# An attention and two-MLP kernel on one core: four query halves with whole float32 weights, a hand-set start, and a new order

## The chip, the cores and the metric

The kernel runs on one core of one Trainium2 chip. The metric is the device time of one execution in microseconds (us). Engines are named as in the profile: PE is TensorE (PEld its weight loads), DVE VectorE, ACT ScalarE, POOL GpSimd, SP SyncE, which here only issues DMAs. Each engine works through its own instructions strictly in the order in which they stand; semaphores hold an instruction until what it reads is there.

## The reference

Sixteen attention problems (2 batches of 8 heads, 768 positions, 64 channels), with a mask made by clustering, then two MLPs over the 1536 tokens:

```
q_assign = argmax(normalised q . normalised centroids)     # 16 clusters a head; the same for k
scores   = where(q_assign == k_assign, q . k / 8, -1e9)
attn     = exp(scores - rowmax) / (rowsum + 1e-9)
x        = attn . v                       # 1536 tokens x 512
x        = elu(x . w_in) . w_out          # 512 -> 2048 -> 512
out      = ((x . w_a) * (x . w_b)) . w_out2     # 512 -> 1536 -> 512
```

Inputs and output are float32. The kernel keeps near-float32 precision by splitting operands into a high and a low part and multiplying the parts. The MLP weights arrive as float64 bits and are made into two float32r parts by steps `wa`, `w0` to `w4`, `wh`, `ws`, `wq`.

## The kernel before

The program is one long table, `ORDER`: each word is a step with its arguments, and the steps are issued in the order of the words. A word such as `tr:0.1.0/tt=1` also names the buffer it takes. So the order of the words is, engine by engine, the order of the instructions; nothing is scheduled at run time.

Heads go in pairs `j` (heads 2j and 2j+1). Queries of a head lie in six tiles `t` of 128; tiles 0 to 2 are half `f`=0, tiles 3 to 5 half 1. For each pair and tile:

- `lk`, `lp`, `lq` load keys, paired queries and single queries; `ka1`, `ka2`, `kb`, `qa`, `qb` make the float32r operands of the scores.
- `sm` multiplies queries and keys with the centroids in plain float32 (12 small products a pair); `m1` to `m5` turn the result into one-hot rows on DVE; `ot`/`oe` (pair 0) or `oh`, `ohs`, `ohd` (the others) put them into rows 64 to 80 of `kb` and `qb`, so that the mask comes out of the score product itself. Ahead of the first `sm` the centroids are loaded (`cn`), normalised (`c0`, `c1`, `c2`), transposed (`c3`) and laid out in blocks (`c4`).
- `sc` makes the scores of one tile (four matmuls of 384 columns), `rm` their row maximum on DVE, `ex` the exponentials on ACT, with row sums. The result `pf` is float32.
- The weights must then be transposed. On one of two paths: `tr` (three PE transposes) with `th`, which copies the transposed tile out of PSUM as a float16 high part, and `tl`, which subtracts for the low part; or `hi` and `lo`, which split `pf` ahead, and `td`, one DMA transpose of both parts. Split tiles go through a ring of four `phl` buffers.
- `av` multiplies with the values in three parts of 12 matmuls: high by high, low value by high, high value by low, 36 matmuls of 384 columns a half, the two heads in the two halves of the array's columns. `v1` and `v2` are the float16 parts of the values. `ra`, `rc`, `rx`, `rb`, `re` bring 1/sum into place and `ev` scales.

`vl` and `vr` load the values and scan them for their largest magnitude. `wm` issues eight warming products of 128 columns that nothing reads. The MLP steps (`h`, `x2`, `ab`, `o` on PE) follow the last attention pair; the first of them, `h:0.0.0`, stands in the table while the last pair is finished.

`av` of half `f` is held by every transposed tile of both heads of that half; `sc` by a free score buffer (two of them), so by `ex` two tiles ago.

Of the kernel before, what the change touches and what calls it, by code (L numbers as in the profile page):

```python
# [76 lines left out]
hi:0.2.1/phl=0 vs:3 w0:1 qb:3.0 sc:1.1/sc=1 wm:54 sc:1.0/sc=0 th:0.0.1.1/pt=0 wm:50 w1:1 kbd:2
lq:6.0/rawq=0 th:0.1.0.1 w2:1 rm:1.1/nm=3 wh:1 lo:0.2.2 rm:1.0/nm=0 ex:1.1/pf=0 ex:1.0/pf=2 wm:59
wm:44 wm:12 tl:0.1.0 vs:1 sc:1.2/sc=1 tr:0.1.1/tt=1 v1:2.1/v1=0 w3:1 lp:2.0/rawp=0 hi:1.1.2/phl=1
lo:1.1.2 sc:0.3/sc=0 v1:1.1/v1=1 wm:9 ws:1 tl:0.0.1 rm:1.2/nm=1 lq:4.0/rawq=1 vs:0 th:0.1.1.0 td:0.2  # L80
ex:1.2/pf=1 rm:0.3/nm=2 tl:0.1.1 tr:1.0.0/tt=0 wm:36 sc:0.5/sc=1 th:0.0.0.1 ex:0.3/pf=0/sum=1 wm:34
tr:1.0.1/tt=1 hi:1.2.1/phl=2 sc:0.4/sc=0 tl:0.0.0 rm:0.5/nm=3 th:1.0.0.1/pt=1 w4:1 tl:1.0.0
# [1076 lines left out]
```

## Time and profile before

| | us |
|---|---|
| median of 3 timed runs | 803.97 (801.41 to 805.08) |
| the profiled execution's own time | 803.56 |
| its span, first to last instruction | 801.8 |
| busy in the span: PE / DVE / ACT / POOL | 786.2 / 580.0 / 414.1 / 355.5 |

The span falls into three stages. Up to the first score matmul operands are loaded and made. Then all four compute engines work on the attention. From the first MLP product on, PE has matmuls back to back. A busy PE is not a PE at its peak, since each matmul's record holds its latency too; what PE has to spare is read from how closely its records follow each other.

### The profile page before, as it was taken

To read this page: it belongs to the slowest core of one execution; us is meant where nothing else is said; L and a number is where in the kernel's file an instruction comes from. 1 tells how busy PE (TensorE), PEld (TensorE's weight loads), DVE (VectorE), ACT (ScalarE), POOL (GpSimd) and SP (SyncE) were. 2 spreads that over 40 slices of the span, in tenths; PEclk is the share of its full clock that TensorE was granted. 3 is DMA by queue.
4 is the path that set the end of the run, shared out by engine and by line. 5 is a ranking of instruction groups with operands and counts; after the bars stand their busy time and mean duration, and the time that the engine had idled before them with its cause. 6 is when DMAs were issued, how large, how long until landed. Compare 5 with 4: busy or idle time off the path is not lost.

```text
span 801.8 us, 11888 instructions
## 1 busy us (share of the span) xinstructions
PE 786.2 (98%) x4474; PEld 645.2 (80%) x4474; DVE 580.0 (72%) x838; ACT 414.1 (52%) x717; POOL 355.5 (44%) x290
## 2 busy tenths in 40 slices
PE   9999999999999999999999999999999999999998
PEld 9877777777778878888888888888888888888886
DVE  4899998899998676987887788874258873565222
ACT  7889998899986443652742654331223323132110
POOL 0688877979853234445444422540133522332000
PEclk9999999999999999999999999999999999999999
DMA  9577999989941113223213220221012211110102
GB/s 311 156 170 165 204 153 202 217 187 159 158 120 46 60 53 105 75 84 104 78 56 105 80 78 27 81 77 54 1 53 76 79 57 52 53 54 0 53 1 105
DMA packets 98009, 79.12 MB, mean 99 GB/s; under 512 B 81248, under 2 KB 81248, under 8 KB 97952
## 3 DMA queue, kind: packets, MB, share of 16 engines
q1 hardware_dynamic: 97648, 77.58, 38.5%
q10 hardware_dynamic: 304, 0.79, 0.3%
q8 instruction: 35, 0.57, 0.3%
q14 instruction: 22, 0.18, 0.1%
HBM read 51.41 MB, written 3.15 MB: 68 GB/s over the span
## 4 chain that ended last, share of the span: by engine, by line
PE 82%; issue 5%; DVE 4%; ACT 3%; DMA 3%; POOL 2%; SPq 1%; POOLq 0%; ACTq 0%; DVEq 0%
PE ab L942 8%; PE ab L943 8%; PE ab L941 8%; PE sc L689 6%; PE x L941 5%; PE h L941 5%; PE h L943 5%; PE x L943 5%; PE h L942 5%; PE x L942 5%; PE o L942 4%; PE o L943 4%; PE o L941 4%; PE av L802 4%; PE tt L743 2%
## 5 line engine op out<-in xcount | busy, mean ns | idle before, releaser
L697 DVE TENSOR_REDUCE nm<-sc 128x1 f32<-128x768 f32 x96 | 90.6, 949 | 6.8 <-PE sc L689 6.3
L725 POOL TENSOR_TENSOR phl<-pf,phl 128x768 f16<-128x768 f32 x49 | 84.2, 1723 | 22.1 <-ACT phl L718 12.7
L710 ACT ACTIVATE pf<-sc,nm 128x768 f32<-128x768 f32 x96 | 86.9, 905 | 10.1 <-DVE nm L697 7.2
L1043 ACT COPY t0ab<-ab 128x512 f32<-128x512 f32 x36 | 21.1, 587 | 109.2 <-PE ab L943 109.2
L1048 DVE TENSOR_TENSOR t1ab<-ab,t0ab 128x512 f32<-128x512 f32 x36 | 24.8, 689 | 63.2 <-ACT t0ab L1043 63.2
L689 PE MATMUL sc<-ka,qa 128*128 128x384 f32 x192 | 59.3, 391 | 4.3 <-ACT pf L710 3.8
L872 ACT ACTIVATE wg<-wraw 128x512 f32<-128x512 f32 x68 | 45.0, 667 | 26.8 <-DMA wraw<-in_w_out_dram 14.4
L802 PE MATMUL av<-pt,v 128*64 128x384 f16 x576 | 54.9, 334 | 0.6 <-DMA qb<-ohs 0.6
L889 DVE SCALAR_TENSOR_TENSOR wf<-wraw,wg 128x512 int32<-128x512 int32 x68 | 51.5, 760 | 1.8
L689 PE MATMUL sc<-kb,qb 80*128 80x384 f32 x192 | 51.0, 347 | 0.4 <-DMA kb<-ka 0.4
L752 DVE TENSOR_TENSOR pt<-tt,pt 128x384 f16<-128x384 f32 x92 | 48.6, 544 | 2.5 <-ACT pt L747 2.3
L902 DVE SCALAR_TENSOR_TENSOR wg<-wraw,wg 128x512 f32<-128x512 uint32 x68 | 49.2, 724 | 1.5
L1059 DVE TENSOR_TENSOR gl<-t1ab,gh 128x512 fp32r<-128x512 f32 x36 | 33.9, 941 | 18.7 <-ACT gh L1054 18.5
L743 PE MATMUL tt<-identf,pf 128*128 128x128 f32 x276 | 44.2, 281 | 2.9 <-DVE pt L752 2.6
L802 PEld LDWEIGHTS <-v 128*64 128x64 f16 x576 | 31.2, 111 | 19.0 <-issue 8.0
L877 DVE TENSOR_SCALAR wg<-wg 128x512 f32<-128x512 f32 x68 | 39.3, 578 | 8.1 <-ACT wg L872 8.0
L689 PEld LDWEIGHTS sc<-ka,qa 128*128 128x128 f32 x192 | 30.1, 195 | 14.5 <-ACT pf L710 11.8
L743 PEld LDWEIGHTS tt<-identf,pf 128*128 128x128 f32 x276 | 32.3, 143 | 11.6 <-DVE pt L752 2.0
L882 DVE TENSOR_SCALAR wg<-wg 128x512 int32<-128x512 int32 x68 | 38.4, 566 | 1.8
L1005 ACT CAST gh<-t1h 128x1024 fp32r<-128x1024 f32 x24 | 25.2, 1052 | 27.6 <-DVE t1h L997 27.6
L997 DVE SCALAR_TENSOR_TENSOR t1h<-t0h,h 128x1024 f32<-128x1024 f32 x24 | 29.2, 1216 | 13.1 <-ACT t0h L992 13.1
L1099 DVE TENSOR_TENSOR acc<-o,acc 128x1024 f32<-128x1024 f32 (+1 forms) x12 | 14.2, 1180 | 32.3 <-PE o L943 32.3
(375 smaller groups left out, 2347.2 us busy)
## 6 DMA issues: line engine op xcount, KB each, us to landing
wraw<-in_w_out_dram SPq DMA_DIRECT2D x28, 512.0 KB, 3.3
wraw<-in_w_in_dram SPq DMA_DIRECT2D x16, 512.0 KB, 3.6
wraw<-in_w_a_dram SPq DMA_DIRECT2D x12, 512.0 KB, 3.5
wraw<-in_w_b_dram SPq DMA_DIRECT2D x12, 512.0 KB, 3.5
rawq<-in_qt_dram SPq DMA_DIRECT2D x30, 192.0 KB, 3.8
rawp<-in_qt_dram SPq DMA_DIRECT2D x8, 384.0 KB, 4.4
acc<-in_v_dram SPq DMA_DIRECT2D x4, 768.0 KB, 11.0
rawk<-in_kt_dram SPq DMA_DIRECT2D x7, 384.0 KB, 5.1
```

What stands on the lines that cost most here:

```text
L689: nc.tensor.matmul(s[:, j, :HALF], a[:, qs], b[:, j * HALF : (j + 1) * HALF], start=i == 0, stop=i == 1,)
L697: nc.vector.reduce_max(out=nm, in_=st[g][f"sc{t}"][:, :, :HALF], axis=AX.XY, negate=True)
L710: nc.scalar.activation(pf.rearrange("p (a b) -> p a b", a=2), st[g].pop(f"sc{t}")[:, :, :HALF], AF.Exp, bias=st[g].pop(f"nm{t}"), accum_ou ...
L725: (nc.vector, None, nc.gpsimd)[e].tensor_sub(phl[:, S:], st[g].pop(f"pf{t}"), phl[:, :S])
L743: nc.tensor.transpose(tt[:, k * P : (k + 1) * P], pf[:, o : o + P], identf)
L752: nc.vector.tensor_sub(lo, st[g].pop(f"tt{t}{u}"), hi)
L802: nc.tensor.matmul(pairs[j]["av"][x * 64 : (x + 1) * 64].rearrange("p (a q) -> p a q", a=3), st[2 * j + x][("v1", "v2")[vi]][:, kt_, :], s ...
L889: nc.vector.scalar_tensor_tensor(out=f, in0=raws[n][:, :, 1], scalar=-0x40000000, in1=g, op0=ALU.bitwise_and, op1=ALU.bitwise_or,)
L902: nc.vector.scalar_tensor_tensor(out=g, in0=raws.pop(n)[:, :, 0].bitcast(U32), scalar=2.0 ** -52, in1=g, op0=ALU.mult, op1=ALU.mult,)
L941: nc.tensor.matmul(ps, lhi, rhi, start=first, stop=False)
L942: nc.tensor.matmul(ps, lhi, rlo, start=False, stop=False)
L943: nc.tensor.matmul(ps, llo, rhi, start=False, stop=last)
```

## The change

- The start of the table is set by hand: the centroid chain comes first, and 12 of the 60 warming steps are left (5 ahead of the first score step where there were 44, 7 behind it where there were 16). Of the 16 value scans, which all stood ahead of the first score step, 13 now stand behind it.
- For the halves in `WHOLE`, that is half 0 of pairs 1, 3, 4 and 6, the transposed weights are kept as one float32 tile. There `th` copies float32, `tl` falls away, all tiles go through PE, and a new step `aw` multiplies them in plain float32 with the float32 values in `acc`: 12 matmuls a half in place of 36. Half 1 of the same pairs sends all six tiles through the DMA transposes.
- `ra` has a second form, on DVE. Casts and other splits move between ACT, DVE and POOL.
- All steps up to the first MLP block stand in a new order.

Counts over the whole table, before and after: `tl` 92 and 52, `tr` and `th` 92 and 100, `hi`, `lo` and `td` 50 and 46, `av` 48 and 36, `aw` 0 and 12, `wm` 60 and 12. By engine: `lo` on POOL 49 and 38, on DVE 1 and 8; `hi` on ACT 38 and 30, on DVE 0 and 5; `qa` on ACT 16 and 9, on POOL 0 and 6; `ra` on ACT 16 and 6, on DVE 0 and 10. From `h:0.0.0` on the products are the same.

```diff
+WHOLE = {(1, 0), (3, 0), (4, 0), (6, 0)}
 ORDER = """
-lk:0.1/rawk=0 wm:0 wm:2 lp:0.0/rawp=0 lq:1.1/rawq=0 cz:0 lq:0.0/rawq=1 ib:0 wm:4 wm:6 cs:0 wm:7
...
+lk:0.1/rawk=0 lp:0.0/rawp=0 wm:0 cs:0 c0:0 md:0 lq:0.1/rawq=0 wm:2 wm:4 c1:0 wl:0 ce:0 ka1:1.1 wa:0
...
     def pt_of(g, f):
         if f"pt{f}" not in st[g]:
-            st[g][f"pt{f}"] = take(ap, "pt", [P, 3, 2 * NT, P], F16, f"pt{f}_{g}", 4)
+            shape, dt = ([P, 3, NT, P], F32) if (g // 2, f) in WHOLE else ([P, 3, 2 * NT, P], F16)
+            st[g][f"pt{f}"] = take(ap, "pt", shape, dt, f"pt{f}_{g}", 4)
         return st[g][f"pt{f}"]
...
     @op
-    def ra(j, f):
+    def ra(j, f, e):
         s = pairs[j]["rs", f] = take(ap, "rs", [P, 16], F32, f"rs_{j}_{f}", 2)[:, :6]
-        nc.scalar.activation(s, flat(pairs[j]["sum", f]), AF.Identity, bias=eps)
+        if e:
+            nc.scalar.activation(s, flat(pairs[j]["sum", f]), AF.Identity, bias=eps)
+        else:
+            nc.vector.tensor_scalar_add(s, flat(pairs[j]["sum", f]), 1e-9)
...
+    @op
+    def aw(j, f, n):
+        if n == 0:
+            pairs[j]["av"] = take(psumA, "av", [P, HALF], F32, f"av_{j}_{f}")
+        for kt_ in (2 * n, 2 * n + 1):
+            for x in range(2):
+                g = 2 * j + x
+                nc.tensor.matmul(
+                    pairs[j]["av"][x * 64 : (x + 1) * 64].rearrange("p (a q) -> p a q", a=3),
+                    staged(g)[:, kt_ * D : (kt_ + 1) * D], st[g][f"pt{f}"][:, :, kt_, :],
+                    start=kt_ == 0, stop=kt_ == NT - 1,
+                )
```

On DVE the centroid chain (`csq`, `cnorm`, `cn`, then `cblk`) stood behind the cast of the identity and a split of keys that waits for ACT. Before:

```order
L408 CAST identb<-identf 128x128
L565 TENSOR_TENSOR ka_243<-rawk_111,ka_243 64x768
L371 TENSOR_TENSOR csq<-cn 128x64
L372 TENSOR_REDUCE cnorm<-csq 128x1
L384 TENSOR_SCALAR cnorm<-cnorm 128x1
L385 RECIPROCAL cnorm<-cnorm 128x1
L386 TENSOR_SCALAR cn_104<-cn,cnorm 128x128
L508 SCALAR_TENSOR_TENSOR qb_304<-rawq_131,qa_291 64x768
L565 TENSOR_TENSOR ka_227<-rawk_111,ka_227 64x768
L508 SCALAR_TENSOR_TENSOR qb_341<-rawq_135,qa_314 64x768
L401 COPY cblk<-cps 64x4x16 x2
```

The same place of DVE after:

```order
L368 TENSOR_TENSOR csq<-cn 128x64
L369 TENSOR_REDUCE cnorm<-csq 128x1
L381 TENSOR_SCALAR cnorm<-cnorm 128x1
L382 RECIPROCAL cnorm<-cnorm 128x1
L383 TENSOR_SCALAR cn_104<-cn,cnorm 128x128
L405 CAST identb<-identf 128x128
L398 COPY cblk<-cps 64x4x16 x2
L562 TENSOR_TENSOR ka_165<-rawk_111,ka_165 64x768
```

The chain is now first, and one cast stands between its scaling and its blocks.

On ACT, at the first exponentials (`pf<-sc`), the value scans (`junk,vmax<-acc`) all stood ahead. Before:

```order
L455 ACTIVATE junk,vmax<-acc 128x384 x6
L558 CAST ka_544<-rawk_455 64x768
L455 ACTIVATE junk,vmax<-acc 128x384 x4
L671 CAST kb_245<-ot_570 16x768
L583 ACTIVATE qa_604<-rawq_513 128x768
L872 ACTIVATE wg_669<-wraw_534 128x512
L583 ACTIVATE qa_674<-rawq_343 128x768
L710 ACT_TABLE_LOAD
L710 ACTIVATE pf_0_677,sum_0_676<-sc_0_622,nm_0_672 128x768
```

ACT at its first exponentials after:

```order
L668 CAST kb_178<-ot_261 16x768
L452 ACTIVATE junk,vmax<-acc 128x384 x3
L707 ACTIVATE pf_0_310,sum_0_309<-sc_0_272,nm_0_298 128x768
L452 ACTIVATE junk,vmax<-acc 128x384
L707 ACTIVATE pf_0_341,sum_0_309<-sc_0_286,nm_0_330 128x768
L452 ACTIVATE junk,vmax<-acc 128x384 x8
L707 ACTIVATE pf_0_409,sum_0_309<-sc_0_375,nm_0_406 128x768
```

Three, one and eight scans now stand around the first three exponentials; the table load has gone further ahead.

On PE, at the products of weights and values of pair 1 half 0 (heads 2 and 3, `pt_2`, `pt_3`), a part was 12 loads and matmuls of float16. Before:

```order
L783 MATMUL rbp_0_1423<-identf,rx_0_1417 128x128 x3
L802 LDWEIGHTS v_2_826
L802 MATMUL av_0_1436<-pt_2_1178,v_2_826 64x384
L802 LDWEIGHTS v_3_1043
L802 MATMUL av_0_1436<-pt_3_1252,v_3_1043 64x384
L802 LDWEIGHTS v_2_1208
```

The same place of PE after, the end of one part and the start of the next:

```order
L818 MATMUL av_0_1051<-pt_3_892,acc 64x384
L785 MATMUL rbp_0_1060<-identf,rx_0_1056 128x128 x3
L686 MATMUL sc_4_1067<-ka_575,qa_632 128x384 x2
L686 MATMUL sc_4_1067<-kb_785,qb_673 128x384 x2
L686 MATMUL sc_4_1084<-ka_575,qa_632 128x384 x2
L686 MATMUL sc_4_1084<-kb_785,qb_673 128x384 x2
L818 MATMUL av_0_1051<-pt_2_776,acc 64x384
```

A part is now four plain float32 matmuls, and scores of pair 2 stand between the parts.

## Rows read from the trace of the kernel before

**Rows 1.** Windows: the stages; busy us (records) by engine, clock, DMA share, GB/s

```profile
0.00:27.20 27.20, 25.75 (x395) 24.91 (x396) 14.06 (x29) 19.06 (x46) 5.70 (x32) 1.00 0.89 293
27.20:236.40 209.20, 199.71 (x1580) 157.10 (x1578) 195.86 (x314) 192.13 (x384) 166.88 (x133) 0.98 0.86 170
300.00:400.00 100.00, 100.00 (x443) 82.81 (x442) 79.13 (x104) 48.15 (x61) 47.52 (x33) 1.00 0.27 86
```

**Rows 2.** Timeline, the first MLP product: start us, duration us, instruction

```profile
236.45 0.48 PE L941 MATMUL h<-x0h,w0h 128*128 128x512 f32 x1
```

**Rows 3.** Timeline, the start: PE, DVE and SP up to the first scores

```profile
0.75 0.40 SPq L354 DMA_DIRECT2D cn<-in_cent_dram  x1
...
1.20 11.09 PE L433 MATMUL warm_ps<-warm 128*128 128x128 bf16 x168 [1.20 <-DVE eps L348]
...
1.35 0.77 DVE L408 CAST identb<-identf 128x128 bf16<-128x128 f32 x1 [0.20 <-POOL identf masks.py:199]
...
7.57 0.23 DVE L371 TENSOR_TENSOR csq<-cn 128x64 f32<-128x64 f32 x1
...
8.70 0.29 DVE L386 TENSOR_SCALAR cn<-cn,cnorm 128x128 f32<-128x128 f32 x1
...
12.12 0.28 PE L395 MATMUL cps<-identf,cn 128*128 128x128 f32 x1
...
12.23 3.74 PE L433 MATMUL warm_ps<-warm 128*128 128x128 bf16 x64
12.51 0.46 DVE L401 COPY cblk<-cps 64x64 f32<-64x64 f32 x2 [0.54 <-PE cps L395]
...
15.81 0.36 PE L602 MATMUL tp<-cblk,rawp 128*128 128x32 f32 x2
...
20.18 0.69 DVE L902 SCALAR_TENSOR_TENSOR wg<-wraw,wg 128x512 f32<-128x512 uint32 x1
...
23.56 0.95 DVE L667 TENSOR_SCALAR qb<-ot 16x768 fp32r<-16x768 bf16 x1 [1.03 <-PE ot L659]
...
27.28 0.59 PE L689 MATMUL sc<-ka,qa 128*128 128x384 f32 x2
```

**Rows 4.** DMA issues of the start: KB each, us from issue to landing

```profile
cn<-in_cent_dram SPq DMA_DIRECT2D x1, 32.0 KB, 3.4
```

**Rows 5.** Groups by line, DVE, 0 to 236.4 us: busy us, mean ns | idle before

```profile
L752 DVE TENSOR_TENSOR pt<-tt,pt 128x384 f16<-128x384 f32 x84 | 44.5, 544 | 0.5 <-ACT pt L747 0.3
...
L767 DVE RECIPROCAL rs<-rs 128x6 f32<-128x6 f32 x15 | 2.7, 181 | 0.0
...
L877 DVE TENSOR_SCALAR wg<-wg 128x512 f32<-128x512 f32 x6 | 2.6, 440 | 0.7 <-ACT wg L872 0.7
...
L725 DVE TENSOR_TENSOR phl<-pf,phl 128x768 f16<-128x768 f32 x1 | 0.9, 939 | 0.0
```

**Rows 6.** Groups by line, ACT, 0 to 236.4 us

```profile
L718 ACT CAST phl<-pf 128x768 f16<-128x768 f32 x38 | 31.6, 832 | 0.3
L583 ACT ACTIVATE qa<-rawq 128x768 fp32r<-128x768 f32 x16 | 13.4, 843 | 0.0
```

**Rows 7.** Groups by line, POOL, 0 to 236.4 us

```profile
L725 POOL TENSOR_TENSOR phl<-pf,phl 128x768 f16<-128x768 f32 x49 | 84.2, 1723 | 22.1 <-ACT phl L718 12.7 <-issue 8.3
...
L718 POOL CAST phl<-pf 128x768 f16<-128x768 f32 x12 | 11.9, 992 | 6.1 <-issue 2.9 <-ACT pf L710 2.8 <-POOL phl L725 0.4
```

**Rows 8.** Chain that ended last, pieces of PE: start us, us

```profile
39.54 0.33 PE tt L743 x3
...
68.17 2.60 PE tp L602 x24
...
124.87 1.10 PE av L802 x12
```

**Rows 9.** Windows, two microseconds behind a `tp` run, columns as in Rows 1

```profile
98.00:100.00 2.00, 2.00 (x13) 0.99 (x13) 1.59 (x3) 1.47 (x4) 1.70 (x2) 0.50 1.07 249
```

**Rows 10.** DMA issues, the transposes: count, us from issue to landing

```profile
pt<-phl SPq DMA_TRANSPOSE x50, 4.2
```

More of the change, by code (lines that the diff above doesn't have):

```diff
@@ L77 @@
[L77 to L82, printed above, removed]
@@ new lines @@
+hi:0.2.1/phl=0 wm:25 vtd:0 ex:1.0/pf=1 kbd:2 ka1:3.2 sc:1.1/sc=1 wa:1 rm:1.1/nm=0 lo:0.2.2
+vbp:0/tt=2 ex:1.1/pf=0 sc:1.2/sc=0 tr:1.0.1/tt=1 vbd:0 sm:1/tt=2 qa:2.1 td:0.2 th:1.0.1.1/pt=1
+th:0.0.1.1 w0:1 rm:1.2/nm=1 vs:0 w1:1 lk:2.0/rawk=0 sc:0.3/sc=1 hi:1.1.1/phl=1 ex:1.2/pf=2 qb:2.0
+sc:0.5/sc=0 w2:1 tl:0.0.1 m1:1/mx=1 rm:0.3/nm=2 lo:1.1.2 vs:1 rm:0.5/nm=3 m2:1 v1:0.1/v1=0
+hi:1.2.1/phl=2 ex:0.3/pf=0/sum=1 m3:1 tr:1.0.0/tt=0 m4:1 v1:1.1/v1=1 ex:0.5/pf=1 lo:1.2.2
+sc:0.4/sc=1 th:1.0.0.1 sc:1.3/sc=0 hi:0.5.1/phl=3 vs:3 rm:0.4/nm=0 lp:2.0/rawp=0 tl:1.0.1
@@ new lines @@
+tl:1.3.1 tr:1.3.0/tt=2 th:0.4.1.1 lq:5.0/rawq=1 tl:0.4.0 hi:1.5.1/phl=2 w4:1 ex:2.0/pf=0/sum=0
+ra:0.1.0/rs=1 v1:2.1/v1=2 ex:2.1/pf=1 lo:1.5.2 sc:2.2/sc=1 tl:0.4.1 rm:2.2/nm=2 wl:2 th:1.3.0.0
+tr:2.0.0/tt=0 tr:2.1.1/tt=1 sc:3.0/sc=0 rx:0.0/rx=0 ka1:5.1 th:2.0.0.1/pt=0 lk:4.0/rawk=1 wq:1
+rb:0.0/tt=0 kbd:4 th:2.1.1.1 ex:2.2/pf=2 tr:2.0.1/tt=1 sc:3.1/sc=1 ka2:5.2 re:0.0.1/rb=0
+tr:2.1.0/tt=0 rm:3.0/nm=3 tl:1.3.0 rc:0.1 ev:0.0 ex:3.0/pf=0 wa:2 rm:3.1/nm=0 th:2.0.1.1 td:1.5 w0:2
+rx:0.1/rx=1 tr:2.2.1/tt=2 th:2.1.0.0 ex:3.1/pf=1 sc:3.2/sc=0 tr:2.2.0/tt=1 th:2.2.0.1 w1:2 kbd:5
@@ new lines @@
+ohd:4 th:7.2.1.1 hi:6.4.2/phl=3 td:6.3/pt=2 ev:2.1 th:7.0.0.0 kbd:10 hi:6.5.1/phl=1 rm:7.3/nm=0
+aw:3.0.0 lo:6.4.2 rm:7.5/nm=3 ex:7.3/pf=1 td:6.4 sc:7.4/sc=1 ex:7.5/pf=0 v2:7.2/v2=3 lp:6.0/rawp=1
+sc:8.0/sc=0 th:7.0.1.1 qa:10.2 lo:6.5.2 hi:7.3.1/phl=0 rx:3.0/rx=0 rm:7.4/nm=2 rm:8.0/nm=1
+ex:7.4/pf=2 vs:11 aw:3.0.1 lo:7.3.0 sc:8.1/sc=1 w4:3 hi:7.4.1/phl=2 ex:8.0/pf=1/sum=0 aw:3.0.2
+ra:3.1.0/rs=1 lo:7.4.2 hi:7.5.1/phl=3 sc:8.2/sc=0 tr:8.0.1/tt=1 v1:8.1/v1=1 rc:3.1 tr:8.0.0/tt=2
+td:6.5 rm:8.1/nm=0 qa:11.0 vs:10 ex:8.1/pf=2 th:8.0.1.1/pt=3 rb:3.0/tt=0 lo:7.5.2 rm:8.2/nm=3
@@ new lines @@
+sc:10.0/sc=0 v2:10.2/v2=1 rm:10.0/nm=1 ex:9.4/pf=2 ka1:12.1 td:8.4 sc:10.1/sc=1 ra:4.1.0/rs=1
+aw:4.0.2 ex:10.0/pf=0/sum=0 lo:9.3.2 re:4.0.1/rb=0 rc:4.1 rm:10.1/nm=0 lq:13.0/rawq=0 sc:10.2/sc=0
+tr:10.0.0/tt=1 ex:10.1/pf=1 w1:4 tr:10.0.1/tt=2 hi:9.4.0/phl=0 rm:10.2/nm=3 th:10.0.0.1/pt=2
+lo:9.4.2 rx:4.1/rx=1 sc:11.0/sc=1 td:8.5 tl:10.0.0 td:9.5/pt=1 tr:10.1.1/tt=0 th:10.0.1.1 td:9.3
+ex:10.2/pf=0 th:10.1.1.1 rm:11.0/nm=2 v2:9.2/v2=2 hi:10.2.2/phl=2 tr:10.1.0/tt=1 sc:11.1/sc=0
+tl:10.0.1 ex:11.0/pf=2 rm:11.1/nm=1 rb:4.1/tt=2 re:4.1.1/rb=1 sc:11.2/sc=1 rm:11.2/nm=0 sm:6/tt=2
@@ new lines @@
+th:10.1.0.1 lo:10.2.2 ev:4.0 v2:11.2/v2=3 ex:11.1/pf=1 hi:11.1.1/phl=3 lo:11.1.2 tl:10.1.0 tl:10.1.1
+ex:11.2/pf=0 hi:11.2.1/phl=1 sc:10.3/sc=0 m1:6/mx=0 td:9.4 ra:5.0.0/rs=0 qa:13.1 m2:6 tr:11.0.0/tt=1
+lk:7.0/rawk=0 sc:10.4/sc=1 tr:11.0.1/tt=0 lo:11.2.2 ka1:13.1 rm:10.3/nm=3 rm:10.4/nm=2 ka2:13.2
+ex:10.3/pf=1/sum=1 m3:6 m4:6 m5:6/oht=0 av:4.1.0 sc:10.5/sc=0 ex:10.4/pf=2 th:11.0.0.1/pt=3 qb:13.0
+sc:11.3/sc=1 rm:11.3/nm=1 hi:10.4.1/phl=0 th:11.0.1.1 oh:6/tt=2 td:10.2 rm:10.5/nm=0 ohs:6/ohs=1
@@ new lines @@
+kbd:12 ex:11.3/pf=0 lo:10.4.2 av:4.1.1 av:4.1.2 td:11.1 ka1:14.2 tr:10.3.0/tt=2 ka2:12.2
+ex:10.5/pf=2 tl:11.0.1 rc:5.0 th:10.3.0.1/pt=0 td:11.2 ohd:6 ev:4.1 sc:11.4/sc=1 tl:11.0.0
+tr:10.3.1/tt=0 sc:11.5/sc=0 rm:11.4/nm=3 av:5.0.0 rm:11.5/nm=2 td:10.4 hi:10.5.1/phl=2
+tr:11.3.1/tt=1 lo:10.5.2 tl:10.3.0 ex:11.4/pf=1 sc:12.0/sc=1 tr:11.3.0/tt=2 th:10.3.1.1 w2:4
+rm:12.0/nm=1 hi:11.4.1/phl=3 lo:11.4.2 tl:10.3.1 av:5.0.1 ex:11.5/pf=2 w3:4 ka2:14.2
+ex:12.0/pf=0/sum=0 th:11.3.1.0/pt=1 lp:7.0/rawp=0 sc:12.1/sc=0 ra:5.1.1/rs=1 rm:12.1/nm=0
@@ new lines @@
+tl:14.0.0 rm:15.0/nm=1 hi:14.2.2/phl=3 th:14.0.1.1 re:6.0.1/rb=0 tr:14.1.0/tt=0 ex:15.1/pf=2
+tr:14.1.1/tt=2 v2:15.2/v2=1 lo:14.2.2 td:13.4 td:13.5 th:14.1.0.1 v2:14.2/v2=3 tl:14.0.1 tl:14.1.0
+sc:15.2/sc=0 ev:6.0 rx:6.1/rx=1 tr:15.1.1/tt=1 rm:15.2/nm=0 ex:15.0/pf=1 th:14.1.1.1 tr:15.1.0/tt=0
+wl:5 sc:14.3/sc=1 th:15.1.1.1/pt=3 av:6.1.0 ex:15.2/pf=0 av:6.1.1 tl:15.1.1 tr:15.0.1/tt=1
+rm:14.3/nm=3 hi:15.2.0/phl=1 sc:14.4/sc=0 th:15.1.0.1 tl:15.1.0 ra:7.0.1/rs=0 tl:14.1.1 th:15.0.1.0
+rc:7.0 lo:15.2.2 ex:14.3/pf=2/sum=1 tr:15.0.0/tt=0 sc:15.3/sc=1 rb:6.1/tt=2 wh:4 tl:15.0.1
@@ L733, in parts_of @@
         f, a = divmod(t, 3)
+        parts = 1 if (g // 2, f) in WHOLE else 2
         return [pt_of(g, f)[:, a, i * NT + 3 * u : i * NT + 3 * (u + 1)].rearrange("p m q -> p (m q)")
-                for i in range(2)]
+                for i in range(parts)]
     @op
```

374 lines of the change are left out of this document (167 added, 207 removed).

## Prediction

> **What bounds the kernel now.** I read the windows by stage first, then the timeline of the start, then the groups by line of each engine, and last the chain of waits for PE's pace. The reader is to see three stages. From the first MLP product at 236.45 us [rows 2] PE has 443 matmuls in every 100 us [rows 1], 0.226 us each, with no gap; these products stay as they are, so what the change gains or loses is how much earlier or later that product starts. From 27.2 to 236.4 us DVE is busy 195.9 of 209.2 us, 93.6%, ACT 91.8%, POOL 79.8% [rows 1]. DVE is the bound there, with ACT close behind. In the first 27.2 us DVE is busy only 14.06 us and ACT 19.06 [rows 1]: that stage is a chain of waits, and 13.1 us of DVE's time are lost in it.
>
> PE shows 199.7 of 209.2 us busy in the attention, but that counts latency. By pace: a score matmul of 384 columns is 0.226 x 384/512 = 0.169 us, a step of three transposes 0.33, an `av` part 1.10, an `sm` 2.60 [rows 8], eight warming products 3.74/8 = 0.47 [rows 3]. From the first score to the first MLP product the table holds 384 score matmuls (65 us), 87 transpose steps (29), 45 `av` parts (49.5), 7 `sm` (18), 15 `rb` at the price of a transpose step (5) and 16 warming steps (7.5): 174 of 209 us, 83%. PE has slack.
>
> **The start.** Today the centroid chain begins at 7.57 us although its data land at 0.75 + 3.4 = 4.15 us [rows 3, 4], because DVE first waits with a split of keys. It then stands before PE, which works off 168 warming products until 12.1 us; the transposed centroids come at 12.12, the blocks are done at 12.97, and `sm` starts only at 15.81, behind 64 more warming products [rows 3]. From there to the first score are 27.28 - 15.81 = 11.47 us.
>
> After: the chain from its load takes 8.70 + 0.29 - 7.57 = 1.42 us to the scaled centroids, 0.28 for the transpose, 0.77 for the cast of the identity that still stands in the way on DVE, 0.46 for the blocks: 4.15 + 2.93 = 7.1 us for `sm`. The 40 warming products left ahead of it end earlier. From `sm` to the first score I take today's 11.47 less two pieces of DVE that now stand behind it, one mask row of `qb` (0.95) and one weight step (0.69) [rows 3]: 9.8 us. First score at 16.9, say 17, where it was 27.3. But work is moved too: DVE's 14.06 us ahead of the score fall to about 10.1 (a split and an operand at 0.95 each, the two pieces above, and 0.4 of the small steps on the value scale). So DVE's idle time at the start falls from 13.1 to 17 - 10.1 = 6.9 us: the start is worth 6.2 us, not 10.
>
> **Work taken off the attention, counted in the table up to `h:0.0.0`.**
> - DVE: 38 `tl` fewer at 0.544 = -20.7; 7 `lo` more at 0.939 = +6.6; 6 `th` more at `tl`'s price (same tile, same PSUM read) = +3.3; 9 `ra` at `rc`'s 0.18 (same six columns) = +1.6; 5 `hi` = +3.3, for which there is no row on DVE: 440 ns for 512 columns gives 0.66 for 768, the split's 0.939 is the upper end, and I take the first as the nearer kind [rows 5]. Six single steps that come or go make about -0.5. Sum -6.4 us.
> - ACT: 8 `hi` at 0.832 and 7 `qa` at 0.843 are 12.6 us less [rows 6]; the moved sums and casts take off some 3 more.
> - POOL: 11 `lo` fewer at 1.723 = -19.0; 6 `qa` more, unseen on POOL, between the cast's 0.99 and the split's 1.72, at 0.99 since it too reads one operand: +6; other moves +1.7. Sum -11 [rows 7].
> - PE: 9 transpose steps more (+3.0), 12 `av` parts less (-13.2), 9 warming steps less behind the first score (-4.2), and `aw`.
>
> `aw` has no row. Twelve plain float32 matmuls of 384 columns a half; the only plain float32 product in the trace, `sm`, shows its 12 as 24 records [rows 8], so 24 records a half. Lower end: a record as cheap as one of `av`, 1.10/12 = 0.092, so 2.2 us a half, 1.1 less than the 3.3 of three `av` parts. Upper end: four column times a record and the two heads one after the other, 24 x 4 x 0.169 = 16.2 us. I take two column times, between one and four, and the heads side by side, as `av`'s row shows it (0.092 against 0.169): 24 x 2 x 0.169/2 = 4.1 us, 0.8 more than today, +3 us in all. PE's sum is then 65 + 31.7 + 36.3 + 18 + 5 + 3.3 + 16.2 = 175 us. Nothing bounds there.
>
> The Trainium skill (FP8 and Floating Point Precision, TensorE Precision Notes) says that true float32 makes 4 passes through the array. By it a half is 12 x 4 x 0.169 = 8.1 us one after the other and 4.1 side by side. No run here shows which; the first is a rival below.
>
> **Sum.** DVE's work to the first MLP product was 14.06 + 195.86 = 209.9; less 6.4 it is 203.5, of which 10.1 stand ahead of the first score. The other 193.4 at today's 93.6% take 206.6 us. 17 + 206.6 = 223.6, against 236.45: 12.9 us earlier. Against that I set 1.5 us for the first tiles, where 13 value scans now stand on ACT among the exponentials; the ends are 0 (the scans hide) and 6.2 (they give the start's gain back). Gain 11.4; the profiled execution's own time 803.56 becomes 792.2, and since the median shown lies 0.4 above it, 792.
>
> What is late next is again DVE, full for 193 of 207 us.
>
> **Rivals.**
> 1. *The start is given back.* Fewer warming products leave PE at the lower clock. The row where the granted clock is 0.50 [rows 9], that is 1.2 GHz, follows an `sm` run and shows DVE at 1.59 and ACT at 1.47 of 2 us. For it: ahead of the first score 39 of 44 warming steps go, 18 of 21 us at 0.47. Against it: at half clock PE's 83% would become a bound only while it lasts, and scores and transposes then keep PE full. Price: the first `sm` takes 2.6 us more and the first tiles about as much again, so the 6.2 us are gone and the work's 6.4/0.936 = 6.8 remain: 797. The Trainium skill (TensorE: Matmul & The Clock Gate, What's actually happening) calls the lower clock the default state, which activity lifts; a start with fewer products has more to fear by that rule.
> 2. *The float32 products stand one after the other.* 8.1 us a half, 4.8 over today's 3.3, so +19 us on PE; its sum becomes 175 + 16 = 191, as long as DVE's 193. Two engines equally full in a fixed order wait for each other; if half of the added 19 shows, the time is 801.6. No change. For it: no row shows two plain float32 products side by side.
> 3. *The DMA transposes come in bursts (slower).* Half 1 of the four pairs sends six tiles through a ring of four buffers. The DMA engines are busy 86% of the attention [rows 1]; 50 transposes in 209.2 us are at most 0.86 x 209.2/50 = 3.6 us of them each, 4.2 from issue to landing [rows 10]. Six take 21.6 us, while six tiles come in 6 x 209.2/96 = 13.1 us: 8.5 us behind in each of four bursts. ACT's next `hi` waits for the ring, and behind it its exponentials. It decides from 11.4/4 = 2.9 us a burst on; if two thirds show, 4 x 5.7 = 23, the time is 803.6 - 11.4 + 23 = 815. Against it: half 0 of the same pairs sends none, and over all there are 46 for 50.
>
> **How the numbers follow.** Forecast 0.58 (own range 786 to 798), rival 1 0.17, rival 2 0.13, rival 3 0.12. About 0.5%, 4 us, is what a measurement of this kernel can tell from no change. Faster by more: 0.55 of the first, 0.15 of the second, a third of rival 2: 0.75. Slower: most of rival 3 and the upper end of `aw`: 0.11. Within: 0.14. Low end of the range: DVE at 96% instead of 93.6 (193.4/0.96 = 201.5, 5 us less), a start at 15.5 and no loss to the scans: 783. High end: rival 2 and the edge of rival 3: 804. Some 0.1 is left out above, 0.06 below.
>
> **What would show it.** Right: the first score near 17 us and the first MLP product near 225; DVE's busy time to there near 203.5 us and still above 92%; `aw` records that overlap in pairs, near 4 us a half; 443 matmuls in 100 us unchanged behind it. Wrong: a clock of 0.50 in many windows of the first 45 us (rival 1); PE without gaps at each `aw` and DVE waiting for scores (rival 2); ACT or POOL waiting for `pt<-phl` in half 1 of pairs 1, 3, 4 and 6 (rival 3).

## The result and the profile after

The changed kernel is slower: 808.39 us median (807.43 to 812.35, 7 runs) against 803.22 (7 runs of the kernel before beside it), a ratio of 1.0075, 95% interval 1.0055 to 1.0095. I had forecast 792. Its profiled execution spans 806.6 us, at a mean granted clock of 0.983 (0.994 before).

Windows of the changed kernel by stage, columns as in [rows 1]: up to the first score, from there to the first MLP product, and 100 us of the MLPs.

```profile
0.00:17.54 17.54, 11.98 (x84) 11.34 (x84) 10.09 (x22) 9.96 (x17) 9.42 (x32) 1.00 0.90 305
17.54:237.99 220.45, 206.32 (x1485) 161.61 (x1485) 201.59 (x307) 190.53 (x392) 161.90 (x129) 0.95 0.82 164
400.00:500.00 100.00, 100.00 (x443) 82.82 (x442) 78.97 (x102) 46.80 (x58) 41.38 (x28) 1.00 0.23 74
```

The first score comes at 17.54 us, as forecast (17), ten microseconds before today's [rows 3]. But the first MLP product comes at 237.99 us, 1.5 us after that of before [rows 2]: 220.45 us lie between them where 209.2 did, with DVE at 91.4% instead of 93.6% and 211.7 us of DVE's work in all, where I had counted 203.5. The MLPs keep their 443 matmuls in 100 us.

Timeline of the changed kernel, PE: the first score, the first MLP product, and a stop inside the first MLP (start us, duration us; in brackets the idle time before and what ended it).

```profile
17.54 1.01 PE L686 MATMUL sc<-ka,qa 128*128 128x384 f32 x2
...
237.99 0.48 PE L956 MATMUL h<-x0h,w0h 128*128 128x512 f32 x1
...
295.17 0.69 PE L956 MATMUL x<-gh,w1h 128*128 128x512 f32 x1 [2.93 <-DVE acc L1044]
```

The last row is a loss that I had not looked for: from the first MLP product to the end the changed kernel takes 806.6 - 238.0 = 568.6 us, before 801.8 - 236.45 = 565.35. PE's wait for `acc` there is 2.2 us longer than the 0.72 us at the same place before, and the matmuls behind it run at the lower clock for a while (0.43 us from start to start instead of 0.23, up to 298.6 us).

Groups by line of the changed kernel up to its first MLP product, DVE, and then POOL (busy us, mean ns | idle before and its releaser).

```profile
L751 DVE TENSOR_TENSOR pt<-tt,pt 128x384 f16<-128x384 f32 x45 | 24.1, 549 | 0.7 <-ACT pt L746 0.6
...
L722 DVE TENSOR_TENSOR phl<-pf,phl 128x768 f16<-128x768 f32 x8 | 8.4, 1051 | 1.0 <-ACT phl L715 1.0
L764 DVE TENSOR_SCALAR rs<-sum 128x6 f32<-128x6 f32 x9 | 6.0, 662 | 0.4 <-ACT pf L707 0.4
...
L715 DVE CAST phl<-pf 128x768 f16<-128x768 f32 x5 | 2.8, 552 | 0.0
L769 DVE RECIPROCAL rs<-rs 128x6 f32<-128x6 f32 x15 | 2.7, 181 | 0.1
```

```profile
L582 POOL TENSOR_SCALAR qa<-rawq 128x768 fp32r<-128x768 f32 x6 | 14.2, 2367 | 7.3 <-DMA rawq<-in_qt_dram 7.3
```

The time of the `tl` went down as counted, from 44.5 us [rows 5] to 24.1. Two prices were wrong by a factor: the small sums `ra` cost 662 ns on DVE, not 180, and a `qa` on POOL 2.37 us, not 0.99.

Windows of the changed kernel: the first `sm`, and the two stretches at the lower clock.

```profile
7.20:12.50 5.30, 5.29 (x27) 5.15 (x24) 3.00 (x5) 3.26 (x5) 3.18 (x2) 1.00 1.04 350
...
29.00:42.70 13.70, 13.70 (x64) 12.89 (x61) 9.91 (x20) 8.68 (x17) 7.74 (x6) 0.50 0.52 136
...
46.10:52.90 6.80, 6.40 (x25) 5.30 (x26) 6.74 (x11) 5.65 (x12) 5.23 (x4) 0.50 0.38 78
```

In the second row PE is full at half speed (0.50, the 1.2 GHz level) and DVE is down to 72%. The kernel before shows a granted clock of 1.00 from 27 to 60 us. The first row reads 1.00 too, but its products run at half pace (see the last section).

### The profile page after: what moved, and what is told of

It reads as the page before. It is cut to its first block, busy times and chain, and to the rows that moved or that the text cites. A ratio compares the mean times of both kernels' runs of the same rounds, so it can differ in the third digit from the quotient of the medians.

```text
span 806.6 us, 10976 instructions
## 1 busy us (share of the span) xinstructions
PE 780.4 (97%) x4066; PEld 637.1 (79%) x4066; DVE 584.8 (73%) x828; ACT 402.0 (50%) x691; POOL 353.5 (44%) x286
## 4 chain that ended last, share of the span: by engine, by line
PE 85%; DVE 5%; ACT 3%; DMA 2%; POOL 2%; issue 2%; ACTq 0%; DVEq 0%; POOLq 0%
PE ab L956 8%; PE ab L958 8%; PE ab L957 8%; PE sc L686 6%; PE h L956 5%; PE h L957 5%; PE h L958 5%; PE x L956 5%; PE x L957 5%; PE x L958 5%; PE o L956 4%; PE o L958 4%; PE o L957 4%; PE av L804 3%; PE tt L742 3%; PE tp L599 3%
## 5 line engine op out<-in xcount | busy, mean ns | idle before, releaser
L722 POOL TENSOR_TENSOR phl<-pf,phl 128x768 f16<-128x768 f32 x38 | 65.3, 1720 | 23.1 <-ACT phl L715 10.3
L917 DVE SCALAR_TENSOR_TENSOR wg<-wraw,wg 128x512 f32<-128x512 uint32 x68 | 52.7, 777 | 1.6
L742 PE MATMUL tt<-identf,pf 128*128 128x128 f32 x300 | 48.9, 287 | 4.9 <-ACT pt L746 1.9
L742 PEld LDWEIGHTS tt<-identf,pf 128*128 128x128 f32 x300 | 37.2, 148 | 14.7 <-issue 3.0
L804 PE MATMUL av<-pt,v 128*64 128x384 f16 x432 | 40.4, 329 | 0.1
L686 PEld LDWEIGHTS sc<-kb,qb 80*128 80x128 f32 x192 | 37.5, 202 | 0.0
L1069 ACT CAST gh<-t1ab 128x512 fp32r<-128x512 f32 x36 | 22.3, 621 | 26.6 <-DVE t1ab L1063 26.6
## 6 DMA issues: line engine op xcount, KB each, us to landing
acc<-in_v_dram SPq DMA_DIRECT2D x4, 768.0 KB, 10.8
```

The lines of the kernel that those rows point to most:

```text
L686: nc.tensor.matmul(s[:, j, :HALF], a[:, qs], b[:, j * HALF : (j + 1) * HALF], start=i == 0, stop=i == 1,)
L722: (nc.vector, None, nc.gpsimd)[e].tensor_sub(phl[:, S:], st[g].pop(f"pf{t}"), phl[:, :S])
L742: nc.tensor.transpose(tt[:, k * P : (k + 1) * P], pf[:, o : o + P], identf)
L804: nc.tensor.matmul(pairs[j]["av"][x * 64 : (x + 1) * 64].rearrange("p (a q) -> p a q", a=3), st[2 * j + x][("v1", "v2")[vi]][:, kt_, :], s ...
L917: nc.vector.scalar_tensor_tensor(out=g, in0=raws.pop(n)[:, :, 0].bitcast(U32), scalar=2.0 ** -52, in1=g, op0=ALU.mult, op1=ALU.mult,)
```

## The experiments

The 13 were timed in four groups (e1 to e4, e5 to e8, e9 to e11, e12 and e13), each in 5 rounds against the kernel before on its own chip, so times of different groups compare by their ratios. "Work" is DVE's busy time up to the first MLP product, and "product" that product's start, both from the one profiled execution; the changed kernel's own product moved by 4.8 us between two such executions of the same attention (e2_tail), so those two columns carry a few microseconds of chance; the ratios carry the intervals shown.

| kernel | median us | ratio to before, 95% | work | product |
|---|---|---|---|---|
| before | 803.2 | 1 | 210.0 | 236.5 |
| changed | 808.4 | 1.0075 (1.0055 to 1.0095) | 211.7 | 238.0 |
| e1_warm | 806.2 | 1.0045 (1.0027 to 1.0064) | 211.9 | 235.1 |
| e2_tail | 804.2 | 1.0025 (1.0002 to 1.0047) | 212.5 | 242.8 |
| e3_qa | 804.8 | 1.0035 (1.0020 to 1.0050) | 206.9 | 235.8 |
| e4_ra | 807.0 | 1.0053 (1.0033 to 1.0073) | 207.4 | 238.8 |
| e5_all | 799.9 | 0.9955 (0.9933 to 0.9978) | 205.7 | 232.8 |
| e6_whole | 828.8 | 1.0333 (1.0305 to 1.0361) | 202.0 | 266.4 |
| e7_cold | 801.8 | 1.0000 (0.9977 to 1.0023) | 210.7 | 237.0 |
| e8_split | 846.9 | 1.0551 (1.0530 to 1.0573) | 238.8 | 274.5 |
| e9_whole_late | 823.7 | 1.0251 (1.0230 to 1.0271) | 201.6 | 255.9 |
| e10_start | 812.2 | 1.0097 (1.0074 to 1.0119) | 213.2 | 247.0 |
| e11_nowarm | 803.0 | 0.9996 (0.9982 to 1.0010) | 203.6 | 237.2 |
| e12_lohi | 812.2 | 1.0118 (1.0082 to 1.0154) | 200.1 | 240.9 |
| e13_best | 803.2 | 1.0010 (0.9992 to 1.0027) | 198.5 | 236.3 |

In all rows but e8_split the work runs from 198.5 to 213 while the product runs from 233 to 266, and the two do not go together: DVE's work alone doesn't give the time. (e8_split, with 27 us more of work, is 36.5 us later.) That is the main finding; what follows is how it came out.

### Four single edits of the changed kernel

**e1_warm.** Warming steps put back in three places.

```diff
-c3:0/tt=0
+wm:16 wm:17 c3:0/tt=0
-ot:2/tt=2
+wm:20 wm:21 wm:22 wm:23 wm:24 wm:25 ot:2/tt=2
-vtp:0/tt=1
+wm:30 wm:31 wm:32 wm:33 vtp:0/tt=1
```

> The changed kernel with 12 warming steps (96 products) put back: 2 ahead of the transposed centroids, 6 between the first score-mask product (sm) and its one-hot transposes, 4 ahead of the transposed value maxima. Theory clock: the changed kernel's PE runs at half pace for sm at 7.2-12.5 us (5.3 us for 2.6) and shows a granted clock of 0.50 at 29.0-42.7 and 46.1-52.9; held at the full clock, those stretches shrink, the first MLP product comes at 230 to 234 us instead of 237.99 and the time is 800 to 805. Rival DVE: DVE's work decides and PE's clock is hidden; the clock rises but the time stays within 2 us of 808.4.

Measured 806.17, ratio 1.0045: some 2.4 us better than the changed kernel, close to the rival. The clock was not held: the first `sm` ran at full speed, but then PE waited 3.35 us for the one-hot rows, and the scores behind the wait ran at half pace (1.01 us for two records, 0.59 once the clock was back). Timeline of e1_warm, PE:

```profile
9.01 2.84 PE L421 MATMUL warm_ps<-warm 128*128 128x128 bf16 x48
15.19 2.09 PE L647 MATMUL ot<-identb,oht 128*16 128x128 bf16 x18 [3.35 <-DVE oht L623]
...
19.53 1.01 PE L677 MATMUL sc<-ka,qa 128*128 128x384 f32 x2
...
25.41 0.59 PE L677 MATMUL sc<-ka,qa 128*128 128x384 f32 x2
```

**e2_tail.** DVE's order at the start of the MLP.

```diff
-wa:13 wa:12 w0:13 w1:13 w2:13 xa:0.0.1 x2:0.1.1 w0:12 xa:0.1.0
+wa:13 wa:12 xa:0.0.1 x2:0.1.1 xa:0.1.0 w0:13 w1:13 w2:13 w0:12
```

> The changed kernel with only the order of DVE at the start of the MLP altered: w0:13, w1:13, w2:13, which wait for a weight load, stand behind xa:0.0.1 and xa:0.1.0 instead of ahead of them. Theory: the 2.93 us in which PE waits for acc at 292.24 and the half-clock stretch behind it go; from the first MLP product to the end 565.3 instead of 568.6 us, time 805. Rival: the wait moves to a later step (the weights 12 and 13 are late for their product), time within 1 us of 808.4.

Measured 804.24, ratio 1.0025. The theory holds: PE's stop is 1.25 us instead of 2.93, the products behind it keep the full pace, and from the first MLP product to the end it is 808.2 - 242.82 = 565.4 us, the number expected. Timeline of the changed kernel, DVE, then of e2_tail, DVE and PE:

```profile
292.27 0.43 DVE L892 TENSOR_SCALAR wg<-wg 128x512 f32<-128x512 f32 x1
...
293.81 1.22 DVE L1044 COPY acc<-x 128x1024 f32<-128x1024 f32 x1
```

```profile
296.97 2.34 DVE L1034 COPY acc<-x 128x1024 f32<-128x1024 f32 x2
299.24 0.41 DVE L882 TENSOR_SCALAR wg<-wg 128x512 f32<-128x512 f32 x1
...
298.33 0.47 PE L946 MATMUL x<-gh,w1h 128*128 128x512 f32 x1 [1.25 <-DVE acc L1034]
```

The two copies that free PE's product buffer now stand ahead of the weight steps. By the middle values two thirds of the changed kernel's loss (0.0050 of 0.0075, the two intervals being about 0.002 wide to either side) are three words in the wrong place, 54 us behind the last thing that the prediction looked at. By the profiles it is rather less: from the product to the end the kernels with the changed order there (changed, e1, e3, e4, e8, e12) take 567.0 to 568.7 us, so 1.6 to 3.3 us more than 565.3.

**e3_qa and e4_ra.** `qa` (16 of 16), or `ra` (16 of 16), on ACT.

```diff
-qa:0.2   qa:1.2   qa:3.2   (and 4 more on POOL or DVE)
+qa:0.1   qa:1.1   qa:3.1
```
```diff
-ra:0.0.0/rs=0   (and 8 more on DVE)
+ra:0.0.1/rs=0
```

> The changed kernel with all 16 scalings of the queries (qa) on ACT, as before; nothing else altered. Theory POOL port: qa on POOL takes 2.37 us and lengthens DVE's instructions beside it (rs<-sum 662 ns, wf 964 for 780, wg 1134 for 684, ka 1321 for 954); without it DVE's busy time to the first MLP product falls from 211.7 to 205-208 us and the time is 803 to 806. Rival ACT: seven more instructions of 0.84 us on ACT, which was idle little, cost more than DVE gains: 809 to 812.

> The changed kernel with all 16 small sums (rs<-sum) on ACT, none on DVE. Theory DVE bound: DVE loses 9 x 0.66 = 6 us of work, the first MLP product comes 4 to 6 us earlier, time 802 to 804. Rival: the 662 ns are time in which DVE waited inside the instruction and is not freed, or ACT takes them up: time within 2 us of 808.4.

e3_qa: 804.78, ratio 1.0035, and DVE's work 4.8 us less (1.8 of them the one `qa` that stood on DVE itself), as the first theory had it. Groups of e3_qa, DVE, up to its first MLP product:

```profile
L754 DVE TENSOR_SCALAR rs<-sum 128x6 f32<-128x6 f32 x9 | 4.5, 502 | 0.8 <-ACT pf L697 0.8
...
L907 DVE SCALAR_TENSOR_TENSOR wg<-wraw,wg 128x512 f32<-128x512 uint32 x5 | 4.1, 827 | 0.0
```

The same groups had 662 and 1134 ns, though nothing was done to them: what changed is what POOL did beside them. One `ra` took 1.61 us in the changed kernel, with POOL at work all through it, and 0.16 us in e3_qa, where POOL stood still beside it. e4_ra took 4.3 us of work off DVE and gained 1.4 to 1.8 us (by median and by ratio), within what chance can do: the rival. The first product did not come earlier (238.84).

### All four together, and the warming

**e5_all and e11_nowarm.** e5_all joins the four edits, with 22 warming steps instead of e1_warm's 12; e11_nowarm is e5_all without the 22.

```diff
-ot:2/tt=2
+wm:20 wm:21 (ten more) ot:2/tt=2
-vbp:0/tt=2
+wm:36 wm:37 vbp:0/tt=2
```

> The changed kernel with the four single edits together (DVE order at the MLP start as in e2_tail, qa and the small sums on ACT) and more warming than in e1_warm: 22 steps, 12 of them between the first sm and its one-hot transposes, where e1_warm left 3.35 us idle and the granted clock fell to 0.50. Theory sum: the four cost different stretches, so they add: 2.2 + 4.1 + 3.6 + 1.4 = 11.3 us off 808.4, 797, and the longer warming another 1 to 3: 794 to 798. Rival overlap: warming, qa and the sums all relieve the same DVE, so that only the largest and the MLP start count: 800 to 804.

> The kernel of e5_all without its 22 added warming steps (the other three edits stay). Theory clock: 2 to 5 us slower than e5_all, 802 to 805. Rival hidden (as e7_cold, where 48 fewer steps cost nothing): within 1.5 us of 799.9.

e5_all: 799.91, ratio 0.9955: it beats both kernels. Windows of e5_all up to and behind the first score:

```profile
0.00:16.42 16.42, 15.22 (x195) 14.95 (x196) 9.06 (x22) 10.10 (x17) 4.97 (x30) 1.00 0.90 301
16.42:232.76 216.34, 204.43 (x1550) 158.98 (x1549) 196.61 (x297) 196.19 (x408) 150.57 (x124) 0.97 0.80 169
```

In ratios it gains 0.0120 on the changed kernel, 9.6 us, where the single edits sum to 0.0142; so they nearly add, and the extra that I expected of longer warming did not come. e11_nowarm at 803.01 (0.9996) puts the warming at 3.3 us: the theory of the clock. By 60 us DVE had done 44.2 us of work in it, and 47.3 in e5_all.

**e7_cold.** The kernel before without 48 of its 60 warming steps.

```diff
-wm:25 ka2:1.0 wm:27 wm:28 c0:0 c1:0 wm:29 wm:26 qa:1.1   (and 44 more)
+wm:25 ka2:1.0 c0:0 c1:0 qa:1.1
```

> The kernel before, with 48 of its 60 warming steps left out and nothing else altered (the first 12 stay). Theory clock: the first scores and transposes run at a granted clock of 0.50 for much of the first 60 us, as in the changed kernel, and the first MLP product comes 3 to 8 us later: 806 to 811. Rival queue: the steps stood ahead of real work on PE (the transposed centroids wait for 168 of them), so that the start is earlier and PE's clock is hidden behind DVE: 798 to 802.

801.78, ratio 1.0000. Window of e7_cold over the first 60 us:

```profile
0.00:60.00 60.00, 43.12 (x309) 36.62 (x309) 43.65 (x80) 48.81 (x101) 31.84 (x52) 0.77 0.72 207
```

The mean clock there is 0.77, and DVE has done 43.65 us of work by 60 us, where the kernel before had done 44.6: nothing is lost that matters. The edit also lets the first score come 1 us earlier (26.26 us), so what shows is the sum of both. In the old order a long stretch at the lower clock cost nothing; in the new one taking out 22 warming steps cost 3.3 us.

### The float32 halves and the start, each alone

**e6_whole, e9_whole_late, e8_split.** The four halves put into the kernel before (e6, e9), and taken out of the changed one (e8).

```diff
 e6_whole, a tile of such a half
-hi:2.2.2/phl=2 ... lo:2.2.2 ... td:2.2
+tr:2.2.0 th:2.2.0.1 tr:2.2.1 th:2.2.1.1      (tl of these halves left out, av -> aw)
 e8_split
-th:2.0.0.1/pt=0
+th:2.0.0.1/pt=0 tl:2.0.0                      (48 times, aw -> av)
```

> The kernel before, with its own start, warming and order, and only the four query halves with whole float32 softmax parts: their 24 tl fall away on DVE, 12 hi, 12 lo and 12 DMA transposes become 24 steps of transposes on PE with 24 copies (20 on ACT, 4 on DVE), 12 av parts become 12 aw. DVE 24 x 0.544 less, 4 x 0.544 more: 10.9 us less of work. Theory DVE bound: at 93.6% that is 11.6 us, time 791. Rival: ACT (now as full) and the ring of pf take it; within 3 us of 802.7.

> As e6_whole (the kernel before with only the four query halves in whole float32), but with the added copies th moved later in the order, half of them some ten steps behind their transpose instead of right behind it. In e6_whole ACT sat idle 23.3 us on these transposes (pt<-tt) and DVE 19.6 us on scores. Theory place: it is the place of the copies in ACT's fixed order that cost e6_whole its 25 us, not the float32 products; ACT's idle time there is about halved and the time falls to 810 to 818. Rival products: the aw or the ring of pf hold PE; 825 to 830 as e6_whole.

> The changed kernel with the four halves in two float16 parts again, all of it through PE: a tl on DVE behind each of their 48 th, 12 av for 12 aw; order and start stay. Theory DVE bound: 48 x 0.544 = 26 us more of DVE's work, at 91.4% some 28 us: 836. Rival: DVE's idle time beside waits for scores and ACT takes part of it: 820 to 828.

e6_whole took 8 us of work off DVE and came out at 828.77, 25.6 us slower; neither theory had that. Groups of e6_whole from 30 to 230 us, ACT, and the same of e9_whole_late from 30 to 250 us:

```profile
L742 ACT COPY pt<-tt 128x384 f32<-128x384 f32 x41 | 18.8, 483 | 23.4 <-PE tt L738 23.3
```

```profile
L742 ACT COPY pt<-tt 128x384 f32<-128x384 f32 x42 | 19.5, 480 | 13.4 <-PE tt L738 13.2
```

In e6_whole each new copy stood right behind its transpose, and ACT, which cannot go past it to the next exponential, sat idle 23 us. With half of the copies some ten steps later that is 13 us, as expected, but the time only fell to 823.7 (I had expected 810 to 818). DVE's waits for scores did not shrink with it (19.6 us in e6_whole, 21.8 in e9_whole_late, in the same windows). The place explains some of it; what holds the rest was not separated. e8_split, at 846.9, is above both of its expectations: 27 us more of DVE's work made 38.5 us, with ACT waiting 38.7 us for row maxima. Both ways steps were put into, or taken out of, an order that was laid for the other form. So e8_split is not the price of two float16 parts, nor e6_whole that of the float32 halves; what the halves are worth in an order of their own was not measured.

**e10_start.** The kernel before with its first 160 steps in the changed kernel's order.

```diff
-lk:0.1/rawk=0 wm:0 wm:2 lp:0.0/rawp=0 lq:1.1/rawq=0 cz:0 lq:0.0/rawq=1 ib:0
+lk:0.1/rawk=0 lp:0.0/rawp=0 wm:0 wm:2 wm:4 cs:0 c0:0 md:0 lq:0.0/rawq=1 c1:0
```

> The kernel before with only its first 160 steps (up to the exponentials of the first head's first three tiles) sorted as the changed kernel has them, engines as before, 27 warming steps for 49 there, the rest of the order untouched. The value scans stand behind the first scores as in the changed kernel. Theory start: first score at 17 to 18 us instead of 27.3 and 5 to 6 us earlier to the first MLP product: 797. Rival given back: the scans and splits that stood in the idle time now stand among the exponentials, the first MLP product comes within 2 us of 236.45: 801 to 804.

812.22, ratio 1.0097, worse than the rival. The first score came at 18.65 us, 8.6 us early, and then a hole opened. Timeline of e10_start, DVE and then ACT:

```profile
30.93 0.96 DVE L687 TENSOR_REDUCE nm<-sc 128x1 f32<-128x768 f32 x1 [6.99 <-PE sc L679]
```

```profile
44.08 0.62 ACT L905 CAST w0h<-wf 128x512 fp32r<-128x512 f32 x1 [5.40 <-DVE wf L879]
```

DVE waits 7 us for the third score: ahead of it PE has transposes of the first two exponentials, and ACT has five value scans before the first of these. The next head's scores stand behind the whole spliced piece, and ACT then sits 5.4 us on a weight step. By 60 us DVE has done 37.5 us of work, before 44.6. So the splice doesn't price the start alone, since it made stalls of its own; what it shows is that an early first score alone need not bring the first MLP product earlier.

### Twelve microseconds off DVE

**e12_lohi and e13_best.** The changed kernel, and e5_all, with 8 `lo` on POOL and 5 `hi` and 2 `v1` on ACT instead of DVE.

```diff
-lo:3.3.0   hi:6.3.0/phl=2   v1:7.0/v1=2
+lo:3.3.2   hi:6.3.1/phl=2   v1:7.1/v1=2
```

> The changed kernel with 8 lo moved from DVE to POOL, 5 hi and 2 v1 from DVE to ACT (as these tiles' kin were before); ra, qa, order, start and float32 halves stay. DVE loses 8 x 1.05 + 2.8 + 0.7 = 11.9 us of work, POOL gains 8 x 1.7 = 13.6, ACT 5.2. Theory DVE bound (the step of the prediction that counts DVE's work): 11.9 x 0.9 = 10 us less, 797 to 800. Rival coupling: each saved us on DVE turns into a wait for scores, since ACT and POOL stand in the same fixed order; within 3 us of 808.4, or slower.

> e5_all with the same 8 lo, 5 hi and 2 v1 taken off DVE. DVE bound: another 8 to 10 us off 799.9, 790 to 792. Coupling: 798 to 804.

e12_lohi: 812.23, ratio 1.0118, 3.8 us slower than the changed kernel, with 11.6 us less of DVE's work; the two intervals overlap (1.0082 to 1.0154, 1.0055 to 1.0095). e13_best: 803.2, ratio 1.0010, 3.3 us slower than e5_all, and there the intervals don't overlap. So DVE's work alone is not the bound. The edit does two things at once, though: what it takes off DVE it gives to POOL (171.3 to 182.4 us up to the product) and ACT (200.5 to 204.0). What the same work would bring if no engine took it was not tried. Waits of the changed kernel from its first score to its first MLP product, DVE and ACT (us in total, times, longest):

```profile
DVE nm L694 <- PE sc L686: 8.7, 15, 1.7
...
ACT pf L707 <- DVE nm L694: 16.5, 22, 3.8
```

The same of e12_lohi:

```profile
DVE nm L684 <- PE sc L676: 17.9, 22, 1.9
...
ACT pf L697 <- DVE nm L684: 12.4, 18, 3.8
ACT pf L697 <- POOL phl L712: 6.0, 7, 1.9
```

DVE waits 9 us more for scores, most of what it was freed of. ACT's exponentials now wait 6.0 us for POOL, 0.8 in the changed kernel: a `lo` at 1.7 us on POOL holds one of the three `pf` buffers longer than one at 1.05 us on DVE. The scores in turn wait for the exponentials, and DVE for the scores. In e13_best ACT waits only 1.5 us for POOL, and DVE 14.7 us for scores (10.3 in e5_all), so this link is not all of it.

## Why the prediction was wrong

**The start: right in place, half in worth.** First score 17.54 us (17 forecast), DVE's idle time ahead of it 7.45 us (6.9). The 17 is in part luck: the first `sm` came at 7.2 us, where the sum had 7.1, but at half pace it took 5.3 us instead of 2.6 (rival 1), and the way from its end to the first score took 5.0 us, where the forecast left 7.2. And by 60 us DVE had done 46.98 us of work against 44.6 before; with 6.2 us gained and 1.5 lost to the scans it should have been 4.7 us ahead, not 2.4. e10_start shows how little the first score says by itself.

**DVE's work: -6.4 us forecast, +1.7 found.** `tl`, `lo`, `th` and `hi` were near their prices: -20.4, +7.5, +2.1, +2.8. `ra` cost 6.0 instead of 1.6. One `qa` on DVE took 1.8 us, and the weight steps `wf` and `wg` grew by 3.4 us with no change of their own; the longest of them, 2.1 and 2.0 us, lie beside POOL's work from end to end. `qb` fell by 2.6 us. I had priced each instruction as if alone.

**ACT and POOL.** ACT fell by 10.8 us, not some 15.6. POOL by 1.3, not 11: `qa` there was 8.3 us dearer.

**`aw`: right.** Timeline of the changed kernel, PE, eight records and sixteen:

```profile
80.13 1.51 PE L818 MATMUL av<-pt,acc 128*64 128x384 f32 x8
...
83.47 2.80 PE L818 MATMUL av<-pt,acc 128*64 128x384 f32 x16
```

Eight more records take 2.80 - 1.51 = 1.29 us, 0.161 each, 3.9 us for the 24 of a half (4.1 forecast). In the trace they start in pairs, one of each head, some 6 ns apart, and a new pair every 0.32 us: two column times, with the heads side by side. Rival 2 is out. So is rival 3: waits for `pt<-phl` are 1.3 us on ACT and 1.8 on POOL in all.

**Rival 1: in part.** The lower clock came, as it was described, and costs 3.3 us in e5_all's order by e11_nowarm, not the whole start.

**The step that failed is the sum:** "The other 193.4 at today's 93.6% take 206.6 us". Both of its terms were wrong. In arithmetic the miss of 12.9 us at the first MLP product (237.99 for 223.6 + 1.5) is 8.8 of more work behind the first score (201.6 us for 193.4, at 93.6%), 0.5 of a later first score, and 3.6 of the lower share (91.4%: 5.1 us, of which I had set 1.5 aside for the scans). So the larger part is the mis-sized work. But the rate fails too: e12_lohi has 200.1 us of work, under my 203.5, and its product came no earlier (240.9), though POOL and ACT had more to do in it. DVE's 93.6% in the kernel before did not carry over to another order. My reading, which the waits of e12_lohi bear out but no run proves, is that it was how well that order fitted these durations: with other durations in another order the same chain, score, maximum, exponential, free buffer, next score, breaks in other places, and work saved on DVE turns into its wait.

**And a place that I did not look at:** "these products stay as they are", I wrote of the MLP, and so they do, but DVE's order between them had changed. That was 1.6 to 3.3 us by the profiles and about 4 in the timing.

Of the 16.4 us between 792 and 808.4, e5_all gets 9.6 back, and each part of it has its own run: DVE's order in the MLP (e2_tail), `qa` on POOL (e3_qa) and the clock (e11_nowarm); `ra` on DVE (e4_ra) is not clear of chance. What stays open is the rest: why e5_all still reaches its first MLP product at 232.8 us and not near 225. By e13_best, taking more work off DVE at POOL's and ACT's cost does not mend it; which link of the chain holds it was not tried, nor was a third score buffer or a fourth `pf`. Nor is it settled what keeps e9_whole_late 20 us slower than the kernel before, when ACT's idle time at the copies is only 13 us.

## What to carry to other kernels

A busy share just under full on one engine, in a program of fixed order, may be a fit and not a rate: test it by taking a known amount of work off that engine before counting on it. Work that is moved between engines must be followed through the buffers that it holds, since a slower engine that keeps a ring slot longer can cost more than the faster one gains (e12_lohi). Price an instruction by what runs beside it, too: here the small sums took four times what they take alone. Compare the order on every engine through the whole program, also where the arithmetic is untouched.
